# A gated mixture of an SSM convolution and an MLP: inverse butterfly in both halves, two spectra sums by accumulating transfers, GpSimd's row arithmetic in one piece, and a new order

## The chip, the cores and the metric

The kernel runs on one NeuronCore of a Trainium2 chip. The metric is the time of one execution on the device in microseconds (us). Before the change, three runs gave a median of 188.55 us (188.06 to 191.26).

The engines of the core run side by side, each through its own list of instructions in a fixed order: TensorE (PE, matrix products), VectorE (DVE), ScalarE (ACT), GpSimd (POOL), and SyncE (SP), which here only issues transfers. POOL issues transfers too: those that add to their destination (accumulating transfers).

## The reference

With S = 2048 rows, D = 640 columns, F = 1536, all inputs in bf16:

```python
g = sigmoid((q * gate_w).sum(-1, keepdims=True))
# A: k shifted by a causal 4-tap filter per column, times v,
#    then a causal convolution over S with ssm_k, done in the reference by FFTs of length 2 S
kv = shift_conv(k, shift_k) * v
y  = irfft(rfft(pad(kv)) * rfft(pad(ssm_k)))[:S] + kv * ssm_D
a  = q * y
# B: an MLP that mixes the rows
h  = layernorm(q)                                # over D
u  = gelu(einsum("sd,sf->df", h, w1) + b1)
b  = (einsum("df,fs->ds", u, w2) + b2).T
out = g * a + (1 - g) * b
```

## The kernel before, in words

Everything lies in SBUF, cut in tiles of 128 partitions. The kernel first records all operations, then emits them in an order that is written out by hand as a list of numbers (`_ORDER`, line 1312), with the PSUM buffer of each group of matmuls (`_SLOTS`). Each engine gets its operations in that order and takes them one after the other; a tracker puts in the semaphore waits that the tiles' reads and writes call for. Nothing is reordered at run time. The helpers `tt` (line 555), `ts` (566), `act` (603), `mms` (630) and `dma` (645) record operations, so that most profile rows have the line of a helper: L559 is any two-input elementwise operation, L298 any matmul, L267 any transfer issued by POOL. Readers must go by the tile names.

The convolution over S is done with a table of Fourier factors in place of an FFT: sequence positions are split in four phases (p = 0 to 3) of each of two halves (h), a small matrix product with the table FTB gives the partial spectra, and butterflies on DVE ("mixing", lines 851 to 875) combine them. The steps:

1. PE transposes ssm_k (tile ssm to wT). A product wT by FTB gives the spectra W of the filter, ACT evicts them from PSUM to C[0] and C[1], DVE mixes them, using the tile SS and others as scratch.
2. The 4-tap filter on k is a matmul with a banded tile: "pp<-KF,KT". kp tiles are k turned for a transposing transfer into KT[0] (rows of the first half) and KT[1] (second half). KT[1] has one extra column of the first half, the halo, which POOL copies from KT[0] (`tensor_copy`, line 1037). ACT evicts the filtered k to ksh[0], ksh[1]; DVE multiplies by v: vkv0 (first half) and kv1 (second half).
3. Products vkv0 by FTB and kv1 by FTB give the spectra A of the data, evicted to C[2] and C[3]. DVE mixes them. For the first half `mixing` does it with two 5120-wide and four 2560-wide operations on DVE; for the second half `mixing_acc` (line 1050) leaves two of the sums to accumulating transfers of 640 KB each, issued by POOL.
4. Spectra are multiplied (`product`, `cross`, lines 1144 to 1193, with further accumulating transfers), the inverse butterflies follow (`invmix`, lines 1196 to 1227), then products with the inverse table GTB (`inverse`, line 1231). Where a half is in `INVE` (line 507), DVE does four more butterfly operations, 128x1280 each (lines 1219 to 1224), and the even phases need half as many matmuls.
5. The MLP: layernorm statistics on DVE, row arithmetic on POOL (`ln_scale`, lines 887 to 912), the normalization of X in place on DVE or ACT (`ln_apply`, line 914; the dictionary `TAKES`, line 715, says which). Then 384 matmuls "X,ring" with w1 into GT through the gelu on ACT, and 384 matmuls "GT,W" with w2. Twelve weight loads ring and twelve W2 go through SP.
6. The gate: products "gq<-X,gwb" on DVE, summed by ACT; small operations for g and 1 - g; at the end out = g a + (1 - g) b, in O1, and the output transfers.

`ln_scale` is done for four blocks of four rows a partition. Its operations are on tiles of 128x4 to 128x16 numbers: gth, gpre, mv, dev, sd, then nm (minus the mean), rstd (a power, on POOL), nm times rstd, and sd times rstd. DVE's normalizations wait for rstd, ACT's for nm; the sd times rstd is wanted only by the gate. The tile dev lies over a part of SS (line 520), so that the mixing may write SS only when dev is done with.

What fixes the order around the change is `_ORDER` alone. In it, POOL's list before is: the row arithmetic of the four blocks, the copy of line 1037 behind three sd operations, one accumulating transfer, the last nm operation (block 0), and all other accumulating transfers.

Of the kernel before, what the change touches and what calls it, by code (L numbers as in the profile page):

```python
# [13 lines left out]
ACT = mybir.ActivationFunctionType  # L14
ALU = mybir.AluOpType
# [425 lines left out]
def _build(nc, A_q, A_k, A_v, A_shift_k, A_ssm_k, A_ssm_D, B_x, B_w1, B_b1, B_w2, B_b2, gate_w, out):  # L441
# [10 lines left out]
    with ExitStack() as es:  # L452
# [51 lines left out]
        c2 = alloc("c2", [128, 16], F32)  # L504
        cst = alloc("cst", [128, 2], F32)
        EVEN = (1,)
        INVE = (1,)
        FALL, GALL = len(EVEN) < 2, len(INVE) < 2
        NF, NGT = 3072 + 1024 * FALL, 3072 + 1024 * GALL
        FTB = alloc("FTB", [128, NF], BF16)  # L510
# [5 lines left out]
        C = [alloc(f"C{i}", [128, 4, 4, D], BF16) for i in range(4)]  # L516
# [12 lines left out]
        kv1 = alloc("kv1", [128, 2, 4, D], BF16, at=E_base)  # L529
# [36 lines left out]
        def ts(eng, o, a, s1, s2, op0, op1=None, mode=1, prio=None, extra=0.0):  # L566
            n = n_of(o)
            d = dve_dur(n, mode) + extra if eng == "DVE" else n / 900.0 + 0.2
            rr = [a] + [x for x in (s1, s2) if isinstance(x, bass.AP)]

            def f(e):
                if s2 is None:
                    return e.tensor_scalar(o, a, s1, None, op0=op0)  # L573
                return e.tensor_scalar(o, a, s1, s2, op0=op0, op1=op1)  # L574
            o_ = SC.add(eng, d, lambda s: T.op(eng, f, rr, [o]), rr, [o], prio=prio, name="ts")
            o_.lock = eng == "POOL" or mode > 1
            return o_

        def stt(eng, o, a, sc, b, op0, op1, acc=None, prio=None):
# [132 lines left out]
            dma(o, i, nbytes, stream=stream, **kw)  # L712

        SSM0 = ((0, 2), (2, 5))
        TAKES = {'wT00': 'ACT', 'wT01': 'ACT', 'wT02': 'ACT', 'wT03': 'ACT', 'wT04': 'ACT', 'ln0': 'DVE', 'ln1': 'DVE', 'ln2': 'DVE', 'ln3': 'DVE', 'ln4': 'ACT', 'ln5': 'DVE', 'ln6': 'DVE', 'ln7': 'ACT', 'ln8': 'ACT', 'ln9': 'DVE', 'ln10': 'DVE', 'ln11': 'ACT', 'ln12': 'ACT', 'ln13': 'DVE', 'ln14': 'ACT', 'ln15': 'DVE', 'kp0': 'DVE', 'kp1': 'DVE', 'wT10': 'ACT', 'wT11': 'ACT', 'wT12': 'DVE', 'wT13': 'DVE', 'wT14': 'ACT', 'kp2': 'ACT', 'kp3': 'DVE'}
        ORDER = "x0 s00 s02 x1 f0 f1 x2 x3 s10 s12 w00 w01 k0 k1 w02 w03 gw t0 t1 v0 v1 k2 k3 v2 v3 t2 t3 w10 w11 w12 w13 g w20 w21 w22 w23".split()
        LNSEQ = "s0 s1 a0 s2 a1 s3 a2 a3".split()
        LB = [0, 4, 8, 12, 16]
# [217 lines left out]
        for h in range(2):  # L936
# [8 lines left out]
            if h == 0:  # L945
# [28 lines left out]
                for w in LNSEQ:  # L974
                    k = int(w[1])
# [64 lines left out]
        fwd_even(srcA, 0, C[2])  # L1040
        for p in (1, 3):
            fwd(srcA, 0, p, C[2], p, 1.0, "A")
        mixing(C[2], C[1], 0)
        for hk in range(2, 4):
            kv(hk)
        srcB = lambda kt, p, ci: kv1[:, kt, p, 320 * ci:320 * ci + 320]
        fwd_even(srcB, 1, C[3])
        for p in (1, 3):
            fwd(srcB, 1, p, C[3], p, 1.0, "A")
        def mixing_acc(R, Th, Ts):  # L1050
            def sl(h, s, n=1):
                return V(h, s * SL, [[1, n * SL]])
# [8 lines left out]
            tt("DVE", V(R, SL, [[-1280, 2], [1, 1280]]), pr(Th, Ts), pr(Th, Ts + 1, True), ALU.add)  # L1061
            tt("DVE", V(R, 0, [[3 * 1280, 2], [1, 1280]]), pr(Th, Ts), pr(Th, Ts + 1, True), ALU.subtract)

        mixing_acc(C[3], C[2], 0)

        for ft in range(FT):
            if ft == 4:
# [15 lines left out]
            if ft in (1, 3, 5, 7):  # L1083
                hk = ft // 2
# [37 lines left out]
                else:  # L1122
                    act(O1[:, 2 * h + j // 4, j % 4, :].rearrange("p (a b) -> p a b", a=2), two, ACT.Identity, bias=c2[:, t:t + 1], scale=omg[:, t:t + 1], vt=vt, name="o1")

        A0 = {0: (C[2], 2), 1: (C[1], 0)}
        A1 = {0: (C[3], 2), 1: (C[3], 0)}
        V0 = {0: (C[0], 2), 1: (SS, 0)}
        V1 = {0: (C[1], 2), 1: (C[0], 0)}
# [31 lines left out]
            tt("DVE", H(dst, 0), H(T0, 0), H(T0, 1), ALU.subtract)  # L1160
            tt("DVE", H(dst, 1), H(T1, 0), H(T1, 1), ALU.add)

        C3a = (C[2], 0)

        def acc_dma(dst, src):
            (hd, sd), (hs, ss) = dst, src
# [29 lines left out]
        def invmix(g, Ya, Yb, sc, bfirst=False, behind=None):  # L1196
            n0 = len(SC.ops)

            def sl(h, s):
                return V(h, s * SL, [[1, SL]])  # L1200

            def pr(h, s, rev=False):
                return V(h, s * SL + (1280 if rev else 0), [[-1280 if rev else 1280, 2], [1, 1280]])
            (ha, sa), (hb, sb), (hs, ss) = Ya, Yb, sc
            for (hy, sy), k in (((hb, sb), 1), ((ha, sa), 0)) if bfirst else (((ha, sa), 0), ((hb, sb), 1)):
                tt("DVE", sl(hs, ss + k), sl(hy, sy), sl(hy, sy + 1), ALU.add)
                tt("DVE", sl(hy, sy), sl(hy, sy), sl(hy, sy + 1), ALU.subtract)
            tt("DVE", sl(ha, sa + 1), sl(hs, ss), sl(hs, ss + 1), ALU.add)
            tt("DVE", sl(hb, sb + 1), sl(hs, ss), sl(hs, ss + 1), ALU.subtract)
            oA = V(hs, ss * SL, [[SL + 1280, 2], [1, 1280]])  # L1210
            oB = V(hs, (ss + 1) * SL, [[-1280, 2], [1, 1280]])
            tt("DVE", oA, pr(ha, sa), pr(hb, sb, True), ALU.add)
            tt("DVE", oB, pr(ha, sa), pr(hb, sb, True), ALU.subtract)
            res = {0: (ha, sa + 1), 2: (hb, sb + 1), 1: (hs, ss), 3: (hs, ss + 1)}


            def q4(h, s, b0, st):
                return V(h, s * SL + b0 * D, [[st * D, 2], [1, D]])
            if g in INVE:
                tt("DVE", q4(ha, sa, 0, 1), q4(ha, sa + 1, 0, 2), q4(ha, sa + 1, 1, 2), ALU.add)  # L1220
                tt("DVE", q4(ha, sa, 2, 1), q4(ha, sa + 1, 0, 2), q4(ha, sa + 1, 1, 2), ALU.subtract)
                tt("DVE", q4(hb, sb, 0, 3), q4(hb, sb + 1, 0, 2), q4(hb, sb + 1, 3, -2), ALU.subtract)
                tt("DVE", q4(hb, sb, 1, 1), q4(hb, sb + 1, 2, -2), q4(hb, sb + 1, 1, 2), ALU.add)
                res.update({0: (ha, sa), 2: (hb, sb)})
            for o_ in SC.ops[n0:]:
                o_.after.update(behind or ())
            return res

        OACC = ()

        def inverse(h, Z):
            for p in (0, 2, 1, 3):
# [77 lines left out]


_ORDER = """
8 0 9 4 10 5 11 7 1 13 12 249 6 26 21 14 20 25 2 32 18 22 16 3 23 17 19 24 33 30 34 31 183 36 35 37 42 185 38 43 44 80
40 39 182 85 83 41 82 79 81 48 84 184 46 78 49 104 52 45 103 54 101 53 107 50 47 86 102 87 64 100 51 88 56 106 55 105
74 153 57 108 70 89 158 65 90 157 76 109 110 154 75 91 58 155 118 92 77 152 111 202 93 156 112 59 113 206 159 94 71
203 160 204 95 207 161 162 200 114 205 163 97 198 201 72 130 164 199 126 115 165 131 116 166 73 127 117 210 119 188
214 211 208 60 132 215 189 167 128 212 99 209 168 220 129 169 133 120 213 216 170 125 134 61 66 122 135 124 221 218
136 123 217 144 222 186 137 223 62 224 187 15 138 219 27 68 253 251 28 252 250 67 171 231 226 63 382 139 69 225 229
232 140 239 230 141 172 237 142 240 181 143 233 179 238 145 190 241 234 388 242 146 175 96 151 176 276 173 149 121 148
150 278 147 192 283 174 389 279 191 383 177 280 277 193 384 178 269 195 281 271 270 194 390 180 272 273 258 385 274  # L1320
196 259 235 386 399 236 197 256 391 282 227 400 228 275 257 260 29 255 254 392 261 288 296 289 290 243 401 297 284 298
285 402 299 292 244 404 293 291 294 415 405 295 263 262 403 286 301 416 325 287 246 327 326 334 328 302 332 335 317
245 333 406 318 300 329 303 330 393 336 304 313 248 337 307 314 305 308 338 315 306 309 316 311 331 310 407 387 440
247 395 418 264 312 339 441 396 408 267 340 319 343 394 442 98 344 353 398 443 397 409 266 351 354 435 320 444 265 345
352 436 346 268 410 437 412 411 347 321 341 348 424 342 429 413 438 355 431 368 322 414 349 425 430 432 350 426 445
427 607 447 323 439 419 433 420 356 428 357 434 366 479 421 602 369 422 480 324 358 423 481 478 417 370 601 359 360
367 451 448 371 361 374 364 372 365 362 373 472 606 375 456 363 446 457 376 449 461 450 609 377 484 471 617 462 604
463 608 603 610 458 612 605 452 473 611 459 616 464 379 453 465 474 460 454 618 378 620 512 455 466 613 485 482 476
381 615 513 491 467 380 492 483 614 486 493 621 494 468 623 514 515 487 495 477 624 469 516 470 541 540 619 488 625
489 622 517 496 518 475 628 526 497 533 527 490 505 519 626 534 520 521 629 627 522 535 523 630 524 506 525 536 635  # L1330
498 528 542 499 500 543 507 636 508 544 501 502 637 529 530 545 643 509 639 537 503 631 531 504 510 633 532 638 538
567 511 632 553 539 642 588 634 568 554 589 569 645 555 570 590 644 556 591 571 650 557 572 648 574 573 575 576 651
581 577 649 582 583 584 653 578 579 652 585 580 586 592 587 686 593 558 594 647 641 640 546 655 646 559 547 658 684
665 687 656 666 659 685 560 657 561 548 654 663 549 689 664 562 677 688 672 660 550 667 678 661 563 690 551 679 668
552 691 564 680 565 673 670 681 692 682 712 662 671 693 696 674 713 698 669 694 697 675 595 699 695 710 566 700 703
711 701 705 717 714 706 702 683 704 715 719 718 707 716 596 720 708 597 598 721 709 676 599 724 600 722 726 723 725
727
"""
_SLOTS = "0123130210230131233001212023123302100321201002022000101003302002112021012002310033002211131230321321203031021123010322003102201130203"
# [1 line left out]
_INS = ['A_q', 'A_k', 'A_v', 'A_shift_k', 'A_ssm_k', 'A_ssm_D', 'B_x', 'B_w1', 'B_b1', 'B_w2', 'B_b2', 'gate_w']  # L1341
_OUTS = [((1, 2048, 640), 'bfloat16')]
# [23 lines left out]
```

## Time and profile before

| | us |
|---|---|
| median of three runs | 188.55 (188.06 to 191.26) |
| the profiled execution | 188.37 |
| its span in the profile | 186.5 |
| PE busy in the span | 172.3, 1356 matmuls |
| DVE busy | 165.9, 174 instructions |
| ACT busy | 111.3, 173 instructions |
| POOL busy | 69.1, 89 instructions |

The span is the time from the first to the last recorded instruction; 1.88 us of the execution lie outside. The profile's second part shows the busy share of each engine in 40 slices of 4.66 us, in tenths; the row PEclk is the clock granted to PE in tenths of full speed. A line of a timeline reads: start, duration, engine, line, operation, output and inputs with their shapes, how many instructions the line holds, and in brackets the idle time before it with what ended it. A duration of a line with several instructions is that of the whole row of them. An instruction's recorded duration holds any time for which it had been started and was held up.

### The profile page before, as it was taken

The numbers are of one execution on the slowest core, as the hardware profiler recorded it, in microseconds if no ns is written. First come the engines' busy times: TensorE is split into PE (matmuls) and PEld (weight loads), VectorE is DVE, ScalarE is ACT, GpSimd is POOL, SyncE is SP. The second block draws the span as 40 slices with busy tenths as digits, with TensorE's granted clock in tenths as the row PEclk, the third lists the DMA queues.
The fourth block names the chain that finished last, engine by engine and source line by source line (L and its number), as shares of the span: only waits on it lengthen the run. The fifth ranks groups of instructions, "written<-read, shape, count | busy, mean of one in ns | idle before, by whom it ended". The sixth has DMA issues, their size and how long they took to land.

```text
span 186.5 us, 3295 instructions
## 1 busy us (share of the span) xinstructions
PE 172.3 (92%) x1356; PEld 134.8 (72%) x1356; DVE 165.9 (89%) x174; ACT 111.3 (60%) x173; POOL 69.1 (37%) x89
## 2 busy tenths in 40 slices
PE   5989689899999999998199999999999999999993
PEld 1756436687679677775057778989999999788672
DVE  2299897699999999942999999999999999999995
ACT  3779899989889999982258040042106015526780
POOL 1797979980000039992003402022039000005500
PEclk9999999999999999999759999999999999999999
DMA  5999989994999989319999978649999998784997
GB/s 189 354 392 400 393 149 187 342 405 154 205 194 355 354 271 289 68 26 180 239 304 319 200 141 187 181 167 202 182 298 252 199 202 163 222 344 76 210 279 280
DMA packets 31658, 44.55 MB, mean 239 GB/s; under 512 B 11673, under 2 KB 21018, under 8 KB 31516
## 3 DMA queue, kind: packets, MB, share of 16 engines
q1 hardware_dynamic: 26384, 33.20, 54.7%
q0 software_dynamic: 5200, 11.14, 33.9%
q8 instruction: 10, 0.16, 0.3%
q14 instruction: 4, 0.03, 0.1%
q10 hardware_dynamic: 60, 0.01, 0.0%
HBM read 27.96 MB, written 2.62 MB: 164 GB/s over the span
## 4 chain that ended last, share of the span: by engine, by line
PE 54%; DVE 14%; POOL 12%; DMA 11%; SPq 3%; issue 3%; ACT 0%; DVEq 0%
PE pp L298 54%; DMA kn<-in_A_k_dram 8%; DVE C L559 7%; POOL nm L559 6%; SPq L272 3%; DMA C<-C 3%; DVE SS L559 2%; DVE kv L559 2%; POOL rstd L559 1%; POOL dev L559 1%; POOL nm L573 1%; POOL gth L559 1%; DVE stats L881 1%; DVE X L574 1%; POOL C L267 1%
## 5 line engine op out<-in xcount | busy, mean ns | idle before, releaser
L559 DVE TENSOR_TENSOR C<-C 128x2560 bf16<-128x2560 bf16 (+2 forms) x41 | 58.0, 1454 | 1.0 <-ACT C L603 0.7
L298 PE MATMUL pp<-X,ring 128*128 128x320 bf16 x384 | 58.2, 303 | 0.7 <-DVE X L574 0.6
L298 PE MATMUL pp<-GT,W 128*128 128x320 bf16 x384 | 54.6, 300 | 0.0
L298 PEld LDWEIGHTS pp<-GT,W 128*128 128x128 bf16 x384 | 51.9, 144 | 1.3 <-ACT O L603 0.4
L298 PEld LDWEIGHTS pp<-X,ring 128*128 128x128 bf16 x384 | 37.4, 99 | 16.2 <-DVE X L574 1.2
L603 ACT ACTIVATE C<-pp 128x640 bf16<-128x640 f32 x64 | 41.3, 725 | 11.5 <-DVE C L559 6.9
L603 ACT ACTIVATE O<-pp,c,omg 128x640 bf16<-128x640 f32 x15 | 12.6, 885 | 26.1 <-PE pp L298 26.1
L603 ACT ACTIVATE GT<-pp,cc 128x640 bf16<-128x640 f32 x12 | 9.6, 802 | 18.2 <-PE pp L298 18.0
L298 PE MATMUL pp<-wT,FTB 128*128 128x320 bf16 x112 | 17.6, 300 | 2.6 <-DVE stats L881 1.1
L267 POOL DMA_DIRECT2D C<-SS x3 | 4.8, 1596 | 34.7 <-DVE C L559 34.7
L881 DVE BATCH_NORM_STATS2 stats<-X 128x6 f32<-128x320 bf16 x32 | 13.0, 478 | 4.3 <-DMA X<-in_A_q_dram 4.1
L603 ACT ACTIVATE cgb<-pp,gg 128x640 bf16<-128x640 f32 x16 | 11.9, 793 | 7.8 <-PE pp L298 5.5
L298 PEld LDWEIGHTS pp<-wT,FTB 128*128 128x128 bf16 x112 | 9.7, 97 | 9.4 <-ACT C L603 3.6
L267 POOL DMA_DIRECT2D C<-C x8 | 10.2, 1887 | 15.5 <-DVE gpre L573 13.0
L267 POOL DMA_DIRECT2D O<-q_hi x4 | 4.8, 1325 | 27.3 <-DVE q_hi L559 27.3
L559 DVE TENSOR_TENSOR tm<-C,C 128x2560 bf16<-128x2560 bf16 (+1 forms) x7 | 14.3, 2059 | 0.0
L298 PE MATMUL pp<-kv,FTB 128*128 128x320 bf16 x48 | 9.7, 335 | 4.8 <-ACT C L603 4.8
L267 POOL DMA_DIRECT2D C<-q_hi x6 | 5.9, 1007 | 21.5 <-DVE C L559 15.8
L559 POOL TENSOR_TENSOR nm<-nm,rstd 128x4 f32<-128x4 f32 x4 | 12.7, 3187 | 0.2
L603 ACT ACTIVATE gq<-gq 128x640 bf16<-128x640 bf16 x16 | 12.0, 766 | 0.8 <-DVE gq L559 0.8
L298 PE MATMUL pp<-C,GTB 128*128 128x320 bf16 x80 | 12.0, 299 | 0.0
L559 DVE TENSOR_TENSOR SS<-C 128x2560 bf16<-128x2560 bf16 x8 | 11.7, 1488 | 0.0
(80 smaller groups left out, 211.6 us busy)
## 6 DMA issues: line engine op xcount, KB each, us to landing
ring<-in_B_w_dram SPq DMA_DIRECT2D x12, 512.0 KB, 9.3
W<-in_B_w_dram SPq DMA_DIRECT2D x12, 512.0 KB, 5.3
C<-C POOLq DMA_DIRECT2D x8, 640.0 KB, 9.9
X<-in_A_q_dram SPq DMA_DIRECT2D x4, 640.0 KB, 10.0
kn<-in_A_k_dram SPq DMA_DIRECT2D x4, 640.0 KB, 13.0
out_dram<-O SPq DMA_DIRECT2D x7, 320.0 KB, 3.2
C<-SS POOLq DMA_DIRECT2D x3, 640.0 KB, 9.7
ssm<-in_A_ssm_k_dram SPq DMA_DIRECT2D x2, 768.0 KB, 9.0
```

Source lines behind the costliest of these rows:

```text
L267: ins = engobj.dma_start(out_ap, in_ap, accum_op=ALU.add, max_dma_last_dim=2560)
L272: ins = engobj.dma_start(out_ap, in_ap)
L298: ins = self.nc.tensor.matmul(ps_ap, lhsT=lhsT, rhs=rhs, start=start, stop=stop, skip_group_check=True)
L559: o_ = SC.add(eng, d, lambda s: T.op(eng, lambda e: e.tensor_tensor(o, a, b, op), rd, [o]), rd, [o], prio=prio, name="tt")
L573: return e.tensor_scalar(o, a, s1, None, op0=op0)
L574: return e.tensor_scalar(o, a, s1, s2, op0=op0, op1=op1)
L603: return T.op("ACT", lambda e: e.activation(o, src, func, **kw), rr + [src], ww)
L881: ops.append(SC.add("DVE", 0.38, (lambda o, i: lambda s: T.op("DVE", lambda e: e.bn_stats(o, i), [i], [o]))(o, i), [i], [o]))
```

## The change

- `INVE` becomes (0, 1): the first half also gets the four DVE operations before its inverse, its even phases take 8 matmuls in place of 16 each, and the table GTB shrinks from 4096 to 3072 columns.
- The first half's spectra go through `mixing_acc` (`PACC = (0,)`): two 5120-wide operations become two 2560-wide differences on DVE and two accumulating transfers on POOL. The scratch of the second half's mixing moves from C[2] to C[1], with the tiles of two later steps (A0, C3a).
- `TAKES` moves one normalization from DVE to ACT (ACT then has seven of 16), and changes which take which; of the last two kp tiles DVE now does the first and ACT the second (before, the other way round); of the W transposes' evictions DVE takes two others.
- The order is new. On POOL all row arithmetic, the last nm among it, stands ahead of the copy of line 1037, and that ahead of every accumulating transfer. On DVE the mixing of W lies between normalizations. On ACT the gelu's table is loaded after another one, where before there was one table load. On SP the load of GTB moves from behind the ring loads to behind the first load of q_lo, which waits for one of the last accumulating transfers.
- Two edits do nothing here: `invmix` can leave sums to transfers for what is in `IACC`, which is empty; and the mark `lock` of `ts` is read when an order is planned, not when a given one is emitted.

```diff
-        INVE = (1,)
+        INVE = (0,1)
...
-            o_.lock = eng == "POOL" or mode > 1
+            o_.lock = eng == "POOL"
...
-        mixing(C[2], C[1], 0)
-        for hk in range(2, 4):
-            kv(hk)
...
-        mixing_acc(C[3], C[2], 0)
+        PACC = (0,)
+        mixing_acc(C[2], C[1], 0) if 0 in PACC else mixing(C[2], C[1], 0)
+        for hk in range(2, 4):
+            kv(hk)
...
+        mixing_acc(C[3], C[1] if 0 in PACC else C[2], 0)
...
-        A0 = {0: (C[2], 2), 1: (C[1], 0)}
+        A0 = {0: (C[2], 2), 1: (C[2] if 0 in PACC else C[1], 0)}
...
-        C3a = (C[2], 0)
+        C3a = (C[1] if 0 in PACC else C[2], 0)
...
+                if (g, k) in IACC:
+                    tt("DVE", sl(tm[g], k), sl(hy, sy), sl(hy, sy + 1), ALU.subtract)
+                    dma(pr(hy, sy), pr(hy, sy + 1), 128 * 5120, stream="POOL", prio=0, accum=True)
+                    su[k], di[k] = (hy, sy), (tm[g], k)
+                else:
+                    tt("DVE", sl(hs, ss + k), sl(hy, sy), sl(hy, sy + 1), ALU.add)
+                    tt("DVE", sl(hy, sy), sl(hy, sy), sl(hy, sy + 1), ALU.subtract)
+                    su[k], di[k] = (hs, ss + k), (hy, sy)
...
+        IACC = ()
...
 _ORDER = """
...
 """
-_SLOTS = "0123130210230131233001212023123302100321201002022000101003302002112021012002310033002211131230321321203031021123010322003102201130203"
+_SLOTS = "0132213033100302230013211302131321210022113030133022000112020303210320121012102103331000021322313100220102313321313000201220121311221"
```

`mixing_acc`, which the first half now calls too:

```python
for i in range(2):
    tt("DVE", sl(Th, Ts + i), sl(R, i), sl(R, 2 + i), ALU.subtract)
    dma(pr(R, i), pr(R, 2 + i), 128 * 5120, stream="POOL", prio=0, accum=True)
tt("DVE", sl(R, 2), sl(R, 0), sl(R, 1), ALU.add)
tt("DVE", sl(R, 3), sl(R, 0), sl(R, 1), ALU.subtract)
tt("DVE", V(R, SL, [[-1280, 2], [1, 1280]]), pr(Th, Ts), pr(Th, Ts + 1, True), ALU.add)
tt("DVE", V(R, 0, [[3 * 1280, 2], [1, 1280]]), pr(Th, Ts), pr(Th, Ts + 1, True), ALU.subtract)
```

## The prediction

> **What bounds the kernel now.** I read the page's first two parts, then the stretch in which TensorE (PE) is not full, then the queue of GpSimd (POOL). The profiled execution took 188.37 us: 186.5 of span and 1.88 around it, 0.2 under the median of 188.55. All sums below are made against 188.37.
>
> ```profile
> PE 172.3 (92%) x1356; PEld 134.8 (72%) x1356; DVE 165.9 (89%) x174; ACT 111.3 (60%) x173; POOL 69.1 (37%) x89
> PE   5989689899999999998199999999999999999993
> DVE  2299897699999999942999999999999999999995
> PEclk9999999999999999999759999999999999999999
> ```
>
> PE and VectorE (DVE) are both near full, with one common hole: DVE's in the 18th and 19th slice (79 to 88 us), PE's in the 20th, and the granted clock falls in the 20th and 21st. The DVE and PE timelines of that place:
>
> ```profile
> 80.00 1.56 DVE L559 TENSOR_TENSOR gq<-X,gwb 128x1280 bf16<-128x1280 bf16 x2
> 87.52 0.83 DVE L559 TENSOR_TENSOR q_hi<-C,C 128x1280 bf16<-128x1280 bf16 x1 [5.97 <-DMA C<-C]
> ...
> 87.20 0.71 PE L298 MATMUL pp<-kv,FTB 128*128 128x320 bf16 x4
> 92.68 1.25 PE L298 MATMUL pp<-kv,FTB 128*128 128x320 bf16 x4 [4.77 <-ACT C L603]
> ```
>
> DVE waits 5.97 us for an accumulating transfer, and PE 4.77 us behind that. The transfer is late because of POOL; its timeline:
>
> ```profile
> 35.53 0.20 POOL L559 TENSOR_TENSOR nm<-nm,rstd 128x4 f32<-128x4 f32 x1
> 35.69 0.33 POOL L573 TENSOR_SCALAR nm<-mv 128x4 f32<-128x4 f32 x1
> 35.99 5.28 POOL L559 TENSOR_TENSOR sd<-sd,rstd 128x4 f32<-128x4 f32 x3
> 41.21 0.27 POOL L1037 COPY KT<-KT 128x20 bf16<-128x20 bf16 x1
> 68.45 1.42 POOL L267 DMA_DIRECT2D C<-SS  x1 [26.97 <-DVE C L559]
> 69.46 12.15 POOL L559 TENSOR_TENSOR nm<-nm,rstd 128x4 f32<-128x4 f32 x1
> 81.56 2.42 POOL L267 DMA_DIRECT2D C<-C  x2
> ```
>
> A row operation of four numbers a partition takes 0.20 us, or 12.15 us. It started at 69.46 and ended when DVE went idle at 81.56: eleven DVE instructions in a row kept it out, and the transfers behind it. The same at 36.66: one sd operation lasts 4.61 us, through three 2560-wide DVE additions. The DVE timeline shows what let it go:
>
> ```profile
> 38.32 2.89 DVE L559 TENSOR_TENSOR C<-C 128x2560 bf16<-128x2560 bf16 x2
> 41.24 2.92 DVE L559 TENSOR_TENSOR C<-SS 128x2560 bf16<-128x2560 bf16 x2
> ```
>
> Between 41.21 and 41.24 DVE had a break of 0.03 us, since the next operation reads what the last one wrote; sd and the copy of line 1037 passed there. So an instruction of POOL passes where DVE idles or breaks, or between two layernorm operations (one each, 35.5 to 36.6), and almost never between two additions: one of 13 such boundaries (29.7) let one through. Issuing a transfer is not held: 1.42 us at 68.45 beside a busy DVE.
>
> **The change part by part.**
>
> *Late nm.* The order puts it with the other row operations. That removes 12.15 us from in front of the transfers of 81.56, and with it the hole: DVE 5.97 us, PE 4.77, and the half clock from 90.71 to 97.54, in which about 2.4 us of PE work were lost. If nothing took their place, PE would gain 7.2, and 2.1 more from the inverse (below): 9.3 us.
>
> *Inverse.* 16 matmuls of 320 columns go: 90.64 us for 644 of them with the half clock give about 0.133 each, 2.1 us. Four 1280-wide DVE butterflies come at a pitch of 0.74: 2.96 us.
>
> *Mixing.* A 5120 addition and subtraction (pitch 2.73 each) become two 2560 subtractions (1.40 each): DVE gains 2.66, and two 640 KB accumulating transfers come. Before, such transfers landed 5.9 to 9.7 us after issue alone, and 3 to 5 us later each when queued. DVE's own sum over the whole kernel hardly moves: -2.66 + 2.96 and a layernorm operation (0.36) moved to ScalarE (ACT), about -0.1. That gives nothing by itself; what counts is where DVE waits. The transfers' cover is DVE's work between their issue and the operation that reads them; where it is shorter than the landing, the rest is a wait (below).
>
> *Row arithmetic first.* In the built order of POOL, nm, sd, nm, sd, sd and then the copy of line 1037 follow the last reciprocal root (rstd), all ahead of every transfer. On DVE the last halves of the W mixing lie between layernorm operations, so the chain to rstd is held by additions. The first of them waits for POOL's last use of a tile that overlays SS; that ended at 33.74 before and, with one addition more in its way, comes about 1 us later (estimate). So DVE is busy from about 34.8 to 41.1 (four additions at 1.40, two layernorm at 0.36), and then waits for rstd. The four steps to its end take 1.7 us unheld (0.29, 0.17, 0.29, 1.05), so rstd ends at R = 41.1 to 42.8; I take 42.5 (before 35.45). The first nm passes beside the layernorm operation that rstd releases. Five remain: sd, nm, sd, sd, copy.
>
> Behind R DVE has no idle time: additions, a kp copy (before, 26.42, a waiting nm did not pass there either), two vkv products and the two 5120 operations, until one break at R + 13.7 = 56.2, where an operation reads its predecessor's result. Before, a break let two operations by. So sd and nm pass, or three; the copy stays. PE comes to the first matmul that reads the copied column at R + 15.8 = 58.3 (it is released by the second vkv product at R + 10.9 and has 29 matmuls at 0.133 and 17 narrow ones at 0.053 ahead). It waits. Behind it stand the rest of the k convolution and all A spectra; DVE runs on until R + 22.3 = 64.8, where the kv product needs ACT's evicted convolution, which needs the blocked matmul. There DVE idles, POOL drains in about 0.8, the copy ends at R + 23.1. PE loses 7.3 us; the clock, which fell 2.8 us after PE went idle before (87.91 to 90.71), takes another 2.4 to 3. DVE idles about 8.2.
>
> The Trainium skill, "SBUF — State Buffer", section "Who interferes with whom", says that a DVE instruction with two SBUF inputs and a GpSimd one that reads SBUF exclude each other for one whole instruction, whoever came first. By that rule the five would pass within five DVE instructions, well before 58.3, and the time would be the 184.8 below. The row of 69.46 (eleven instructions, 12.15 us) speaks against it, and I go by the row.
>
> *The first half's sums.* The operation that reads both accumulated halves (T87) needs the second new transfer, which POOL issues after the second subtraction. Without a stall DVE does kv product, subtraction, gq, kv product, subtraction from R + 22.3 on (four at 1.40 and one at 0.74): 28.6, issue at 29, and landing 7.0 later, as three of before did (5.9 to 9.7): R + 36.0 = 78.5. With it the row starts only after the copy (R + 23.1), 63 narrow and 4 wide matmuls (3.9 us, at half clock for most of it 7) and an eviction: R + 30.5, so that issue is at R + 37.4 and T87 = R + 44.4 = 86.9. DVE has three more gq products and C3's even sums to do meanwhile, under 6 us, so the landing ends last in both.
>
> *From T87 to the end.* Before, DVE worked 95.4 us from 87.52 to 184.35 (96.8 less 1.4 idle). After it there are now also: sum and difference of the mixing 2.80, three gq products 2.22, four butterflies 2.96; the second half's even sums, 2.14, are done before. 95.4 + 5.8 = 101.2, with 1.0 for waits 102.2. The end lies 2.14 after DVE's last operation, and 1.88 outside.
>
> *Small ones.* A second ACT table load (1.28 us, one before) lies ahead of ssm's landing at 19.4: 0 to 1.3, taken 0. GTB's load moves behind the q_lo load, which waits for a late accumulating transfer; by the landing times it is there 0 to 1.5 us after the operation that readies the inverse's first operand: inside the 1.0. Behind it on the DMA queue of SyncE stand the q_hi loads, wanted only after the first inverse matmuls. DVE's wait for the last products' transfers: 0 to 2.8, also there. One layernorm more on ACT (0.92) has ACT's idle time at 40 to 60 as cover.
>
> Sum: 86.9 + 102.2 + 2.14 + 1.88 = 193.2 us. With R from 41.1 to 42.8, a stall 1 us shorter or longer and waits of 0 to 2.8 it is 190.5 to 196.
>
> **The rivals.**
>
> A: the halo copy gets by. All five pass at the break of 56.2 or at boundaries before it, as the 13th did; it decides at 58.3, PE's arrival. Then 78.5 + 102.2 + 4.0 = 184.8 (182 to 188): faster. For it: sd and copy both passed in a break of 0.03 us. Against: only two were pending, and eleven boundaries let nothing by at 69 to 81.
>
> C: the copy passes late but before 64.8, or DVE breaks a second time near 60: at 60 to 63, a stall of 1.7 to 4.7 us whose longer cases also halve the clock: 184.8 plus 1.7 to 6, so 188.5 (186 to 191).
>
> D: the copy is in time and the new transfers are late instead. Queued behind the other transfers, the second lands 9.7 after issue, T87 = R + 38.7: 187.4. It lies in A's and C's range and has no chance of its own. PE or the table GTB as the bound: PE then needs 4 to 5 us less than DVE, so no.
>
> E: nothing gained or lost, since the hole at 82 goes and DVE's sum is the same: that needs a stall of about half B's; it is C.
>
> **How the numbers follow.** The forecast, the stall (B), 0.55; A 0.33; C 0.12. I take B's 193.2. Its own range is 190.5 to 196. The range 183.5 to 196 leaves out A's lower third and B's edge, about 0.15. A difference of 2% (faster below 184.8, slower above 192.3) is about what a measurement of this kernel can tell from no change. B gives 0.39 slower, 0.16 same; A half faster, half same; C same: faster 0.16, same 0.44, slower 0.40.
>
> **What would show it.** In the new profile's POOL timeline: an sd or nm of over 10 us ending near 56, another ending near 65, the line-1037 copy after it; in PE's, an idle time of about 7 us from 58 with releaser POOL KT, the clock digit below 9 in the 14th and 15th slice; DVE idle about 8 us before a kv product; no hole at 82 to 93; 16 matmuls fewer; T87 near 87. The forecast is wrong if POOL's row operations all end before 57, or if PE reaches the copied column later than 64.8 for another reason, or if DVE's part behind T87 is not 102 us.

## The result, and the profile after

The changed kernel takes 187.69 us, the median of 20 runs (184.54 to 189.65), against 189.42 (187.62 to 191.26, 20 runs) before. The ratio is 0.986, interval 0.982 to 0.990. A ratio here compares only those executions of each kernel that lie within 1.5% of its fastest (7 of 20 of the changed kernel, 2 of 6 of the kernel before with nm early), so the medians of all executions stand beside it; by them the ratio is 0.991. So in these runs the kernel is faster by 0.9 to 1.4%, less than the 2% that was set as a clear difference. The prediction said 193.2 and slower.

The profiled execution took 188.27 us, of which 186.5 are span. TensorE (PE) starts an execution at one of two paces, in both kernels (last section); this one has the slow start and the profiled one of before the quick one, so the two profiles are compared part by part and not by their spans.

The page of the changed kernel, first and second part:

```profile
PE 172.9 (93%) x1340; PEld 134.1 (72%) x1340; DVE 165.4 (89%) x177; ACT 113.2 (61%) x175; POOL 75.7 (41%) x91
PE   6969988999996999999699999999999979999992
DVE  2299299799999996799999799999998989999994
PEclk9999999999999999999999999999999999999998
```

The common hole of before at 79 to 93 us is gone, and with it the fall of the clock. PE has smaller gaps instead, one at 59, one at 92 and one at 149 us. The GpSimd (POOL) timeline leads to the first:

```profile
41.08 2.25 POOL L559 TENSOR_TENSOR nm<-nm,rstd 128x4 f32<-128x4 f32 x1
43.28 13.62 POOL L559 TENSOR_TENSOR sd<-sd,rstd 128x4 f32<-128x4 f32 x1
56.85 0.19 POOL L559 TENSOR_TENSOR nm<-nm,rstd 128x4 f32<-128x4 f32 x1
57.00 2.85 POOL L559 TENSOR_TENSOR sd<-sd,rstd 128x4 f32<-128x4 f32 x2
59.79 0.86 POOL L1037 COPY KT<-KT 128x20 bf16<-128x20 bf16 x1
```

One sd operation lasts 13.62 us, to the break at 56.83, as forecast (56.2). Behind the break the rest does not stay: two more pass at 58.3 and 59.7, each with the start of a VectorE (DVE) instruction, and the copy of the halo column (line 1037) ends at 60.65. PE and its gaps:

```profile
57.98 1.01 PE L298 MATMUL pp<-KF,KT 128*128 128x128 bf16 x17
60.71 1.45 PE L298 MATMUL pp<-KF,KT 128*128 128x96 bf16 x26 [1.73 <-POOL KT L1037]
...
93.26 4.93 PE L298 MATMUL pp<-X,ring 128*128 128x320 bf16 x35 [1.58 <-DMA ring<-in_B_w_dram]
```

And the chain that ended last, from the break on:

```profile
59.85 0.82 POOL KT L1037
60.67 0.05 issue
60.71 4.89 PE pp L298 x75
65.61 0.03 issue
65.64 15.17 PE pp L298 x108
...
81.30 11.91 DMA ring<-in_B_w_dram
93.22 0.05 issue
93.26 46.91 PE pp L298 x344
140.18 0.02 issue
140.19 10.29 DMA W<-in_B_w_dram
150.48 0.05 issue
150.53 32.47 PE pp L298 x236
```

PE waits 1.73 us for the copy, not 7.3, and sets the end: the chain runs through PE and two transfers. The first is the reload of the w1 tile "ring". It can start only when PE has read the old tile for the last time, at 80.80, lands 11.9 us later, and is waited for. In before the same reload was issued in parts at 54, 59, 67 and 90 us, and PE waited for none of it.

### The profile page after: what moved, and what is told of

Read it like the earlier page. It is cut to its first block, busy times and chain, and to the rows that moved or that the text cites. A ratio compares the mean times of both kernels' runs of the same rounds, so it can differ in the third digit from the quotient of the medians.

```text
span 186.5 us, 3270 instructions
## 1 busy us (share of the span) xinstructions
PE 172.9 (93%) x1340; PEld 134.1 (72%) x1340; DVE 165.4 (89%) x177; ACT 113.2 (61%) x175; POOL 75.7 (41%) x91
## 4 chain that ended last, share of the span: by engine, by line
PE 62%; POOL 16%; DMA 14%; DVE 4%; ACT 1%; issue 1%; ACTq 0%; DVEq 0%; SPq 0%
PE pp L298 62%; POOL sd L559 10%; DMA ring<-in_B_w_dram 6%; DMA W<-in_B_w_dram 6%; POOL nm L559 2%; DMA rows<-in_A_shift_k_dram 2%; DVE stats L881 2%; POOL rstd L559 1%; ACT wT L603 1%; POOL mv L573 1%; POOL gth L559 1%; DVE kp L694 1%; DVE wT L613 1%; POOL nm L573 1%; POOL dev L559 0%
## 5 line engine op out<-in xcount | busy, mean ns | idle before, releaser
L559 DVE TENSOR_TENSOR C<-C 128x2560 bf16<-128x2560 bf16 (+2 forms) x47 | 61.2, 1345 | 1.1 <-DMA C<-SS 0.6
L298 PE MATMUL pp<-X,ring 128*128 128x320 bf16 x384 | 55.6, 299 | 2.0 <-DMA ring<-in_B_w_dram 1.6
L298 PE MATMUL pp<-GT,W 128*128 128x320 bf16 x384 | 53.7, 299 | 1.1 <-DMA W<-in_B_w_dram 1.1
L298 PE MATMUL pp<-wT,FTB 128*128 128x320 bf16 x112 | 19.7, 324 | 3.1 <-ACT wT L603 2.1
L267 POOL DMA_DIRECT2D C<-C x10 | 12.6, 1853 | 20.5 <-DVE C L559 17.5
L559 POOL TENSOR_TENSOR sd<-sd,rstd 128x4 f32<-128x4 f32 x4 | 17.9, 4487 | 0.0
L267 POOL DMA_DIRECT2D C<-q_hi x6 | 6.4, 1146 | 25.9 <-DVE c L559 14.7
L603 ACT ACTIVATE gq<-gq 128x640 bf16<-128x640 bf16 x16 | 11.9, 744 | 0.9 <-DVE gq L559 0.9
L603 ACT ACTIVATE ksh<-pp 128x1024 bf16<-128x1024 f32 (+1 forms) x12 | 11.0, 949 | 1.4 <-PE pp L298 1.4
L267 POOL DMA_DIRECT2D C<-SS x3 | 5.3, 1769 | 13.6 <-DVE C L559 13.6
L298 PE MATMUL pp<-KF,KT 128*128 128x128 bf16 (+1 forms) x160 | 9.0, 213 | 1.8 <-POOL KT L1037 1.7
```

The lines of the kernel that those rows point to most:

```text
L267: ins = engobj.dma_start(out_ap, in_ap, accum_op=ALU.add, max_dma_last_dim=2560)
L298: ins = self.nc.tensor.matmul(ps_ap, lhsT=lhsT, rhs=rhs, start=start, stop=stop, skip_group_check=True)
L559: o_ = SC.add(eng, d, lambda s: T.op(eng, lambda e: e.tensor_tensor(o, a, b, op), rd, [o]), rd, [o], prio=prio, name="tt")
L603: return T.op("ACT", lambda e: e.activation(o, src, func, **kw), rr + [src], ww)
```

## The experiments

Theory 1: the change removes the hole, and gets back into three new waits of PE (copy, w1 reload, w2 reload) most of what that gave. Theory 2: VectorE's list, which is about as long as before, sets the end, and PE's waits cost nothing. Each ratio below is to the kernel before, with its interval; behind it stand the medians of all executions, the kernel's and that of before measured beside it. "Wide" are 320-column matmuls, counted in the PE timelines up to 48.0 us; idle is PE's behind 48 us, added up; these and the span are of the one profiled execution of each kernel.

| kernel | ratio | medians | span | wide by 48 us | idle |
|---|---|---|---|---|---|
| before | 1 | 189.42 | 186.5 | 188 | 5.1 |
| changed | 0.986 (0.982 to 0.990) | 187.69 / 189.42 | 186.5 | 153 | 4.4 |
| changed, again | 0.992 (0.987 to 0.997) | 190.01 / 189.00 | 190.3 | 168 | 7.0 |
| copy ahead | 1.003 (0.999 to 1.007) | 189.86 / 189.00 | 188.1 | 154 | 4.8 |
| three more operations | 1.008 (1.002 to 1.013) | 192.94 / 189.00 | 192.5 | 154 | 8.4 |
| before, nm early | 0.961 (0.954 to 0.968) | 184.45 / 189.00 | 183.0 | 167 | 0.2 |
| reload early | 0.979 (0.971 to 0.986) | 187.49 / 188.93 | 183.8 | 167 | 3.8 |
| reload early, copy ahead | 0.986 (0.981 to 0.992) | 186.83 / 188.93 | 183.7 | 167 | 3.4 |
| reload and GTB early | 0.989 (0.983 to 0.996) | 186.65 / 189.72 | 185.6 | 155 | 3.3 |
| sums on VectorE | 0.982 (0.976 to 0.989) | 186.56 / 188.93 | 182.5 | 169 | 2.5 |
| the same, inverse as before | 0.986 (0.981 to 0.991) | 186.37 / 189.72 | 184.7 | 172 | 3.3 |
| one table load | 0.982 (0.972 to 0.991) | 189.26 / 188.93 | 188.8 | 154 | 5.4 |
| all mended | 0.978 (0.973 to 0.984) | 184.98 / 189.72 | 183.1 | 167 | 2.9 |
| before, nm early, 11 zeros | 0.969 (0.963 to 0.974) | 183.02 / 189.72 | 180.9 | 181 | 0.2 |
| before, 11 zeros | 1.000 (0.996 to 1.003) | 188.68 / 189.47 | 186.3 | 185 | 4.7 |
| changed, 11 zeros | 0.987 (0.983 to 0.991) | 187.76 / 189.47 | 185.1 | 165 | 4.9 |

In the diffs, `move(a, b)` takes operation a out of the written order and puts it right behind b (`move(a, b, 0)`: right ahead of b). `...` marks lines left out.

**The changed kernel again.** No edit.

> The changed kernel as it is, as the base for the others. If the four GpSimd row operations pass in the same way in each execution (the first at the break of VectorE near 56.8 us, then one at each following boundary), the halo copy ends at 60 to 61 us again, TensorE waits 1.5 to 2 us for it, and the ratio to the kernel before is 0.98 to 0.99. If the passing is a matter of chance, the copy ends anywhere between 57 and 66 us, and the wait is 0 to 7 us.

Its profile has no wait for the copy: nm passed one boundary earlier, the other operations one or two at each boundary behind it, and the copy was done at 43.97. Yet it is the longer one, 190.3 us. What it gained at 58 us it lost at the reload, and more (PE timeline):

```profile
90.74 7.26 PE L298 MATMUL pp<-X,ring 128*128 128x320 bf16 x40 [2.58 <-DMA ring<-in_B_w_dram]
100.85 0.37 PE L298 MATMUL pp<-X,ring 128*128 128x320 bf16 x1 [2.85 <-DMA ring<-in_B_w_dram]
```

40 wide matmuls take 7.26 us here, where 35 took 4.93 above: behind the longer wait the granted clock is 0.50 at 92 to 94 us. The last part of the reload, issued at 80.63, landed 20.2 us later. So the passing differs between executions of the same program, and of these two the one with the held copy was the shorter. The medians of this series, 190.01 and 189.00, show no gain of the change at all.

**The copy ahead of the four row operations.**

```diff
+        move(ktc, nms[2])      # ktc: the copy of line 1037; nms[2]: the nm that follows rstd
```

> The changed kernel with the halo copy ahead of the four row operations that wait for nobody. Theory 1 (the copy's place in GpSimd's queue sets TensorE's wait, and TensorE sets the end): the copy passes at the break near 56.8 us, the wait of 1.73 us for it is gone, and 1 to 1.7 us of the time go with it. Theory 2 (VectorE runs back-to-back there and sets the end): the wait is gone too, TensorE waits for something else later, and the time changes by less than 0.4 us.

The copy itself was held (43.10, for 13.70 us) and passed at the break, in time; the wait for it is gone. Both theories missed: nothing was gained. The ratio, 1.003, lies above the changed kernel's 0.986 and 0.992, but the medians of all executions measured side by side are equal (189.86 and 190.01), so that a loss is not shown. The waits of PE say where the 1.7 us went: 3.3 us for ring, 1.6 in the first profile of the changed kernel, and the clock falls behind it.

```profile
PE pp L298 <- DMA ring<-in_B_w_dram: 3.3, 2, 2.7
PE pp L298 <- ACT wT L603: 2.1, 3, 1.2
PE pp L298 <- DVE dif L573: 1.7, 1, 1.7
PE pp L298 <- DMA W<-in_B_w_dram: 1.3, 1, 1.3
```

**Three more row operations ahead of the copy.**

```diff
+        more = [tt("POOL", dum[:, 4 * i:4 * i + 4], mv[:, 0:4, 0], rstd[:, 0:4], ALU.mult) for i in range(3)]
+        order[at:at] = [o_.idx for o_ in more]      # at: the copy's place
```

> The changed kernel with three more row operations of 128x4 (their results are not used) on GpSimd ahead of the halo copy. Theory 1 (after a break one row operation passes at each boundary between VectorE instructions): the copy ends three boundaries later, at 64 to 65 us, TensorE waits 5 to 6 us, its granted clock falls, and the time is 4 to 8 us longer than that of the changed kernel, as the prediction priced its stall. Theory 2 (VectorE alone sets the end, and it is held only by what the copy delays): 0 to 3 us longer. If all pass at once where one passes, the copy stays at 60 to 62 us and the time is the same.

One passes at each boundary, the copy ends at 64.71, and the forecast's stall is there (POOL, then PE):

```profile
59.65 3.58 POOL L559 TENSOR_TENSOR dum<-mv,rstd 128x4 f32<-128x4 f32 x3
63.18 1.53 POOL L1037 COPY KT<-KT 128x20 bf16<-128x20 bf16 x1
```

```profile
64.76 4.55 PE L298 MATMUL pp<-KF,KT 128*128 128x96 bf16 x47 [5.94 <-POOL KT L1037]
```

DVE idles 6.63 us, T87 (the operation that reads both accumulated halves) comes at 86.44 (forecast 86.9), the granted clock is 0.50 from 63 to 69 us, and the profiled execution takes 194.34 us. The stall's price was right in this execution; its condition was not met by the changed kernel. By the medians (192.94, and 190.01 of the changed kernel beside it) the three operations cost 2.9 us, the upper end of theory 2 and less than theory 1's 4 to 8.

**The kernel before with nm early, and nothing else.**

```diff
+        move(nms[0], ktc)
```

> The kernel before with one edit: the last nm operation stands ahead of the first accumulating transfer on GpSimd, directly behind the halo copy. Theory 1 (nm made the hole at 82 to 93 us): the transfers issued at 81.6 us are issued at 69 to 76, VectorE's wait of 6.0 us, TensorE's of 4.8 us and the fall of the clock behind it go, and the time is 4 to 8 us shorter: shorter than the changed kernel's. Theory 2 (the hole is only one of several waits, TensorE or VectorE is bound right behind it): 0 to 2 us shorter.

3.9% faster by the ratio, 2.4% by the medians, and faster than the changed kernel by both. Its page and PE's waits:

```profile
PE 174.0 (95%) x1356; PEld 136.1 (74%) x1356; DVE 165.3 (90%) x174; ACT 111.4 (61%) x173; POOL 57.8 (32%) x89
PE   5989978999999999999999999999999999999991
```

```profile
PE pp L298 <- DVE zz L628: 2.0, 1, 2.0
PE pp L298 <- ACT wT L603: 1.9, 2, 1.1
PE pp L298 <- ACT C L603: 0.6, 4, 0.2
PE pp L298 <- DMA W<-in_B_w_dram: 0.2, 1, 0.2
```

With the hole gone PE is full from 32 us to the end. So moving one operation of 0.2 us is worth more than the whole change, and the rest of the change costs 1.5 to 2.6% (0.991 against 0.976 by the medians, 0.986 against 0.961 by the ratios). The section's theory 2 fails here: VectorE is as busy as in the changed kernel (165.3 and 165.4 us), both profiles have the slow start, and this span is 3.5 us shorter.

**The reload of w1 early.** Blocks 3 and 7 of the first MLP product change places, since block 3 is the last reader of the tile; the reload follows.

```diff
+        for i in range(5):      # four groups of matmuls and the gelu
+            a, b = order.index(m1[3][0] + i), order.index(m1[7][0] + i)
+            order[a], order[b] = order[b], order[a]
...
+        order = [i for i in order[:at + 1] if i not in loads] + loads + [i for i in order[at + 1:] if i not in loads]
```

> The changed kernel with two column blocks of the first MLP product swapped in place (block 3, the last reader of the first w1 ring tile, comes where block 7 was, with its buffer), and the reload of that tile right behind: on the same queue, but released some 6 us earlier (75 in place of 81 us). Theory 1 (the forecast gain went into the wait for this reload, which stands behind the accumulating transfers): TensorE's waits for ring, 1.6 to 5.4 us in three profiles of the changed kernel and its variant, fall under 0.5 us, and the time is 2 to 5 us shorter than that of the changed kernel (ratio to the kernel before 0.96 to 0.98). Theory 2 (VectorE's list is as long, and sets the end with or without this wait): under 1 us shorter.

The reload is issued at 71.0 and PE waits for ring no more. But the time is only 0.979 (it overlaps the changed kernel's interval), because the waits move on: the accumulating transfer issued at 70.4 now shares the 16 DMA engines, busy throughout from 74 to 80 us, with the reload. It lands 9.7 us later, and DVE waits for it, which it did not in the changed kernel (issued at 73.0, the row that reads it started at 80.10 unwaited); further on PE waits for GTB. From the waits of PE and of DVE:

```profile
PE pp L298 <- ACT C L603: 2.4, 6, 1.6
PE pp L298 <- ACT wT L603: 2.2, 3, 1.2
PE pp L298 <- DMA GTB<-gtab: 1.8, 1, 1.8
```

```profile
DVE C L559 <- DMA C<-C: 3.6, 1, 3.6
```

**The reload early and the copy ahead.** Both edits together.

> The same with the halo copy ahead of the four row operations too. Theory 1: with the ring wait out of the way, the 1.7 us that TensorE waits for the copy count: 0.5 to 2 us shorter than with the ring edit alone, in executions in which the copy is held. Theory 2: the same time as with the ring edit alone.

0.986; its interval overlaps that of the reload alone (0.971 to 0.986), and the medians are 186.83 and 187.49: no gain, as in theory 2. In this profile, as in that of the reload alone, the copy was not held (done at 41.50), so that the 1.7 us could not show.

**GTB early too.**

```diff
+        move(toks["g"], SC.ops[loads[-1]])
```

> The changed kernel with the earlier reload of w1 and with the load of GTB behind that reload, ahead of the w2 loads, where it waits for nobody. Theory 1 (TensorE waits for GTB, 1.8 us in the profile of the earlier reload): that wait goes, and 1 to 1.8 us of the time. Theory 2 (VectorE, late by the 3.6 us that it waits for an accumulating transfer, readies the first operand no earlier): under 0.5 us, and TensorE waits for ScalarE or VectorE there instead.

Theory 2 here: the wait for GTB is gone, PE waits for ScalarE's results there (2.6 and 0.8 us), DVE still for the transfer (3.8), and the ratio, 0.989, is no better than 0.979.

**The two sums on VectorE.**

```diff
-                dma(pr(R, i), pr(R, 2 + i), 128 * 5120, stream="POOL", prio=0, accum=True)
+                if dve:         # true for the first half
+                    tt("DVE", sl(R, i), sl(R, i), sl(R, 2 + i), ALU.add)
+                else:
...
```

> The changed kernel with the two sums of the first half's spectra done by VectorE (two additions of 2560, 2.8 us more) in place of the two accumulating transfers. Theory 1 (the transfers crowd the queue ahead of the ring reload): the reload lands 2 to 4 us earlier, TensorE's wait for ring falls under 1 us, and the time is 0 to 2 us shorter in spite of VectorE's 2.8. Theory 2 (VectorE sets the end): 2 to 3 us longer.

No wait for ring, none of DVE for the sums, 0.982: within the interval of the changed kernel, though DVE has 2.8 us more to do. The reload was issued at 78.6 to 80.9 us, later than in the repeated run (77.4 to 80.6), and was in time all the same: without the two transfers it landed sooner. What they save VectorE, 2.8 us, it lost again where the reload was early (3.6 us of waiting).

```profile
PE pp L298 <- ACT C L603: 1.2, 6, 0.4
PE pp L298 <- DMA W<-in_B_w_dram: 1.2, 1, 1.2
PE pp L298 <- DVE kv L559: 0.7, 1, 0.7
```

**The same without the first half's inverse butterfly.** `INVE = (1,)`, its four operations taken out of the order.

> The changed kernel with the first half's two sums on VectorE and without its inverse butterfly (four VectorE operations of 0.74 us fewer, 16 matmuls and a table of 4096 columns more), so that two parts of the change are undone. Theory 1 (with the sums on VectorE no transfer is waited for, and TensorE is full to the end): 1.5 to 2.5 us longer than with the sums alone on VectorE, whose profile has a span of 182.5 us. Theory 2 (VectorE sets the end): 1 to 3 us shorter.

The profile's PE ends 2.2 us later (181.22, not 178.98): 16 matmuls more (2.1), 0.8 of idle more (this copy was held, 1.7), 0.4 less still to do at 48 us, 2.5 together. The intervals of the ratios, 0.986 and 0.982, overlap, and the medians are 186.37 and 186.56; that the butterfly gains is seen in the matmuls of one profile, and not shown by the times.

**One table load.** `move(tbl, cwo, 0)`: the gelu's table ahead of the first copy out of PSUM.

> The changed kernel with one table load on ScalarE, as in the kernel before: the table of the gelu is loaded before the first copy out of PSUM. Theory 1 (the load delays the first eviction of wT by 1.3 us, and with it the spectra of the filter): TensorE's waits for ScalarE's wT (2.1 us) fall by 1 to 1.3, and the time by 0.5 to 1.3 us, unless the ring wait takes it. Theory 2 (the ssm transfer and VectorE's statistics come later anyway): the same within 0.4 us.

The wait for wT stays at 2.1 us, which is theory 2; the time cannot tell, since PE waits 4.0 us for ring in this profile. The second load costs nothing that can be measured.

**All mended.** The sums on VectorE, reload, GTB and copy early, one table load, 11 matmuls on zeros.

> The changed kernel with all that cost it something mended: the sums on VectorE, the reload of w1 earlier, GTB earlier, the halo copy ahead, one table load, 11 matmuls on zeros. Theory 1 (these were the waits that took the gain): TensorE waits for no transfer but w2, the span is 180 to 182 us, under that of the kernel before with only nm moved (183.0). Theory 2 (other waits take their place): 183 to 186.

183.1 us of span, theory 2; 0.978, no lower than with the reload alone (0.979), and still behind the kernel before with nm early. It shows where the rest lies. Against that kernel with the same start (180.9), by the table: 14 wide matmuls fewer by 48 us, at 0.133, +1.9; 16 fewer in all, -2.1; idle +2.8 (its waits are w2 1.6, VectorE's kv 0.8, ScalarE 0.6): +2.6. PE's last matmul ends at 179.60 against 176.98: +2.6.

**The start.** `NSPIN = 11` in place of 7: matmuls on zeros ahead of all work, in three kernels.

> The kernel before with the early nm, and 11 matmuls on zeros at the start in place of 7. Theory 1 (in some executions TensorE works at half its pace up to 16 to 18 us because its busy start falls badly in the interval by which its clock is set: 128-column transposes in groups of eight take 1.07 in place of 0.71 us): with a longer start all executions are of the quicker sort, 181 to 182 us, and the spread falls under 1.5 us. Theory 2 (the difference has another cause): the spread stays at 4 us, and the time is 0 to 1.5 us longer.

> The kernel before with 11 matmuls on zeros at the start in place of 7, and nothing else: with the early nm this made all executions start TensorE at its full pace. Theory 1 (half of the difference between executions is this start): 187 to 190 us, spread under 2 us, no execution with the slow start. Theory 2: spread as before (187.6 to 191.4), time 0 to 2 us longer.

> The changed kernel with the same 11 matmuls. Theory 1 (the change's gain of 1.4% was measured over a mixture of starts; with the quick start TensorE comes earlier to the ring reload and waits for it longer, as in the profile of the repeated run, 5.4 us): 186 to 189 us, ratio to the kernel before 0.985 to 1.0, TensorE's waits for ring 3 to 6 us where the halo copy is not held. Theory 2 (the start is worth as much here as anywhere): 184 to 186 us, and waits for ring under 2 us.

With nm early the runs lie between 181.8 and 183.6 (181.1 to 185.1 without); the kernel before, between 188.2 and 190.7 (187.6 to 191.3), a spread of 2.5 us where theory 1 said under 2. The changed kernel still spreads from 185.3 to 189.8; that its copy, held in one execution and not in another, makes this spread is not shown. Its profile has the copy held and waits 1.6 us for ring. Its ratio stays 0.987, and the medians with 11 zeros are 187.76 and 188.68. So what the change gained, 0.5 to 1.3% here, does not come from the start; and moving nm alone still gains 3.0% (183.02 against 188.68).

## Why the prediction was wrong, point by point

- *Late nm, and the hole.* Right, and more than the whole gain. Its size was forecast as 7.2 us; with the same start, 11 zeros, it is 5.4 us of span (186.3 to 180.9) and 5.7 of the medians.
- *R, and the held sd.* Right in the main, with some luck: rstd ended at 41.00, 1.5 us sooner than taken and just outside 41.1 to 42.8, but VectorE did not wait for it, and two additions put the layernorm operation at 43.19 (42.5 forecast). One operation was held to the break at 56.83 (56.2), and PE reached the copied column at 59.0 (58.3).
- *"So sd and nm pass, or three; the copy stays."* This step failed. Behind the break one operation passes at every boundary: three of three here and in the run with 11 zeros, six of six with three operations more. The copy ended at 60.65, not at 65.6, and PE lost 1.73 us to it, not 7.3 and the half clock. That is rival C's place (60 to 63) and price (186 to 191), to which 0.12 was given; 188.27 was measured in that execution. In seven of the twelve profiles of the changed kernel and its variants the copy was not held at all, done by 46 us: rival A's condition, but not its time, since the reload took what was gained (192.15 us in the repeated run). That the median, 187.69, lies between A and C is luck: neither sum has the waits that made it. I had taken the closed boundaries of the nm at 69.46 as the rule (nine between ten instructions, miscounted as eleven) and the 0.03 us break as the exception; the state behind a break is a third case that the trace of before shows only once, at 29.7.
- *The stall's price.* Right in the one profile that has such a stall: with three operations more, T87 is at 86.44 (86.9) and the profiled time 194.34 (190.5 to 196).
- *The inverse.* 1340 matmuls in place of 1356, as forecast. 90.64 / 644 is 0.141, not 0.133; at the full clock 40 wide matmuls took 5.43 us, 0.136 each, so 2.2 us.
- *From T87 to the end.* 102.2, and 2.14 behind VectorE: 104.3 to the end of the span. Measured 186.5 - 80.10 = 106.4. Sized 2 us too low: PE ended the chain, and not VectorE.
- *"PE or the table GTB as the bound ... so no."* Failed too. I compared sums of work and not the order of PE's list: the w1 reload, which before stood at 54 to 90 us, was moved behind PE's last use of the tile, and I followed SyncE's queue for GTB alone. That wait (1.4 to 5.4 us, with the half clock behind the longer ones) and the one for w2 (1.1 to 1.6) took what the copy left. The 16 matmuls saved at the end are matched by 14 to 20 fewer done by 48 us (changed 153 and 168, the kernel before 167 and 188, slow and quick start). For the quick start the traces show where: PE waits 1.21 us for the first wT, where before it waited 0.24 for FTB, and the granted clock is at half for 3.41 us behind that. The first products of wT in before and in the repeated run:

```profile
10.15 0.30 PE L298 MATMUL pp<-wT,FTB 128*128 128x320 bf16 x1 [0.24 <-DMA FTB<-ftab]
11.03 6.16 PE L298 MATMUL pp<-wT,FTB 128*128 128x320 bf16 x43 [0.58 <-ACT wT L603]
```

```profile
11.30 0.30 PE L298 MATMUL pp<-wT,FTB 128*128 128x320 bf16 x1 [1.21 <-ACT wT L603]
12.13 7.19 PE L298 MATMUL pp<-wT,FTB 128*128 128x320 bf16 x39 [0.53 <-ACT wT L603]
```

39 matmuls at the pace of before would take 5.6 us, so the half clock costs 1.6 us, 12 matmuls. The wait is as long with one table load; what of the new early order makes it, no experiment took apart, nor why the slow start loses 14.

- *The rule on the port.* The Trainium skill, "SBUF — State Buffer", section "Who interferes with whom", has a loser blocked for one instruction; behind a break that is what the traces show (one per boundary), and in the repeated run nearly so (one or two), but the 13.62 us through eight boundaries are not. Neither the rule alone nor my row alone gives the time.

## What to carry to other kernels

When a change removes a wait, follow each queue that it reorders to the next transfer that needs a buffer released by the engine that now runs ahead: here the wait only moved, from the copy to the reload, and from the reload to an accumulating transfer. Try the smallest part of such a change alone first: one operation of 0.2 us, moved, was worth 2.4 to 3.9%, and the rest took 1.5 to 2.6% back. Work given to transfers is not free when a reload needs the same DMA engines.

## What the runs showed of the hardware

A small GpSimd operation beside a busy VectorE behaves in two ways. In all twelve profiles of the changed kernel and its variants the same nm operation starts some 0.7 us into the same 1.40 us addition. In seven it passes at the next boundary, and then all that follow pass too, one or two at each; in five it misses, passes with the next layernorm operation, and the one behind it is held for 13.6 us, to the first break. In both cases the successor starts some 0.1 us behind the start of a VectorE instruction: in the seven an addition of 1.40 us, at whose end it passed; in the five a layernorm operation of 0.36 us with an addition behind it. What decides the first case was not found.

TensorE starts at one of two paces. Eight transposes took 0.71 us at 5.5 us in before and 1.07 in the changed kernel, with the same instructions and a granted clock that the page shows as full in both (the same group of PE's timeline in both):

```profile
5.50 0.71 PE L298 MATMUL pp<-ident,ssm 128*128 128x128 bf16 x8
```

```profile
5.39 1.07 PE L298 MATMUL pp<-ident,ssm 128*128 128x128 bf16 x8
```

The list of granted clocks in the traces tells the two apart. It begins with the first grant of the full clock, at 5.3 us in before and at 17.7 in the changed kernel; the time ahead of it has no entry, and the page shows that as full. Of the twelve profiles with seven matmuls on zeros, seven have the first grant at 4.5 to 5.4 us and five at 16.9 to 17.7. The late one costs 15 to 21 wide matmuls by 48 us (before 188, and 167 with nm early; changed 168 and 153), 2.0 to 2.8 us. With four more matmuls on zeros the first grant came at 5.0 to 8.0 us in all four profiles, and the transposes ran at 0.71 from the second group on at the latest.

An early grant is not always kept. In the seven changed kernels with the quick start and no row operations added, the clock falls to half for 3.41 us at 11.3 to 12.2 us; with three row operations more it falls at 8.2 for 10.24 us, and that start counts as slow in the table (154). In the kernel before it holds.

In all sixteen profiles the stretches between two changes of the clock last a multiple of 3.41 us, but for the last one, which the end cuts off: 3.41, 6.83, 10.24, 85.33 and so on. The Trainium skill, "TensorE: Matmul & The Clock Gate", Part 1, puts the warm-up down to a free-running window of 3.4 us, so that it depends on where in it the work falls; the multiples and the two paces of the same program agree with that. That the clock stays at half up to 17.7 us in the changed kernel, with PE busy 1.85 to 2.00 us of every 2 from 4 to 12 us, does not follow from the length of the window, and no run here explains it.
